# Filter spectrum first, kv spectrum second: swapping two transforms of an FFT-free long convolution and multiplying straight out of PSUM

## The chip, the cores and the metric

One core of one Trainium2 chip runs the whole program. The metric is the device time of one execution in microseconds (us); lower is better. Times are medians over several executions; the profile comes from one of them.

## The reference, cut to what matters

```python
def _A_ref(q, k, v, shift_k, ssm_k, ssm_D):           # S = 2048 rows, D = 576 columns
    k_shift = sum of 4 shifted copies of k, each times a row of shift_k
    kv = k_shift * v
    kv_f = rfft(pad(kv, 2*S), axis=rows)
    kf_f = rfft(pad(ssm_k, 2*S), axis=rows)            # the filter
    y = irfft(kv_f * kf_f)[:S].astype(bf16)
    return q * (y + kv * ssm_D)

h = layernorm(A_q) * (1 + ca) + sa                     # ca, sa, ... = silu(c) @ w_mod
x = A_q + ga * _A_ref(h, A_k, A_v, ...)
h = layernorm(x) * (1 + cb) + sb
x = x + gb * ((silu(h @ w1) * (h @ w3)) @ w2)          # F = 4608
```

The inputs are bf16. Both transforms need the same matrix of cosines and sines, 2048 x 2048 each.

## The kernel before, in words

The real FFTs are done as matrix products. Rows are cut into T = 16 blocks of 128 (index `a`, time) and 16 blocks of 128 frequencies (index `b`); a quad `bq` is four frequency blocks, 512 columns. The cosine and sine tiles `tq_c[a]`, `tq_s[a]` (128x512) are computed on the chip. One **generation**, for one `a` of one quad, is `gen1` and `gen2` (lines 124 to 141): ACT computes `g_y`; DVE computes `g_q`, `g_frs`, `g_m` and `g_frc`; ACT takes two sines into `tqx_s` and `tqx_c`. There are 4 x 16 = 64 generations. Each finished tile is also written to DRAM (`TC_dram`, `TS_dram`), from where the later stages load it again in halves of 128x256.

The stages follow one another on PE in this order.

1. Setup (lines 74 to 212): constants, the product `modps` of silu(c) with `w_mod`, its rows `B1row`, `A1row` and so on copied out of PSUM by DVE, then broadcast rows `skb`.
2. **X** (lines 282 to 348): the transform of `kv`. `x_gen(0)` makes the first quad's tiles. Then a loop over `a` makes `kv[:, a, :]` (lines 316 to 336): four loads `ktile`, four products and three additions on DVE, one load `vtile` from the POOL queue and a last product. `nyquist_pass(kv)` follows on PE, then `x_compute` for each quad: for each `b`, 64 matmuls of 288 columns accumulate into four PSUM tiles (`acc_c` and `acc_s`, two halves of D each, two buffers per tag, so all eight banks). DVE copies `acc_c` to `PX` and ACT copies `acc_s` to `SX` (lines 308 and 309). Generations of the next quad run under the matmuls, in a second buffer of tiles.
3. **LN1** (lines 354 to 363): the first layernorm, 16 rows of tiles, all on DVE with a square root on ACT, written to `H1_dram` from POOL.
4. **F** (lines 371 to 404): the transform of the filter. The filter is loaded transposed into `filtT` by 16 DMA transposes (lines 374 to 376), although an earlier `filtT` was loaded in the same way at lines 338 to 340; that first copy is read by nobody. `nyquist_pass(filtT)` follows, then for each pair of frequency blocks 32 loads of `tqf_c`, `tqf_s` from DRAM and 64 matmuls for each `b`. `pointwise` (lines 249 to 266) multiplies the two spectra: ACT scales the four PSUM tiles into bf16 `cfw`, `sfw`, and DVE makes six operations on 128x576 bf16 to give `YR` and `YI`.
5. The inverse transform (lines 408 to 452), with the gates, the second layernorm and writes to `H2_dram`.
6. The feed-forward part (lines 458 to 525).

A tile framework puts each engine's instructions into one fixed order, by priorities and a model of its own, and adds semaphore waits for data and for reused buffers. Each engine runs its list in order. DMAs are issued from the lists of SP, ACT or POOL; a DMA whose wait isn't met holds up all that stands behind it on that engine. Hardware-queue DMAs share eight completion semaphores in rotation, and software-queue DMAs (from POOL) another eight, so a DMA also waits for the one that used its semaphore before. PSUM and SBUF of a closed pool are reused by the next one, whose first writer waits for the old readers.

Of the kernel before, what the change touches and what calls it, by code (L numbers as in the profile page):

```python
# [20 lines left out]
def kernel(  # L21
# [26 lines left out]
    T = S // P  # L48
# [182 lines left out]
    filtT = fltp.tile([P, T, D], BF16, name="filtT")  # L231

# [16 lines left out]
    def pointwise(b, acc_c, acc_s, pw):  # L249
        wc = w_col0 if b == 0 else w_col  # L250
        cfw = pw.tile([P, D], BF16, name="cfw")
        sfw = pw.tile([P, D], BF16, name="sfw")
        for h in range(2):
            hs = slice(HOFF[h], HOFF[h] + HSZ[h])
            nc.scalar.activation(out=cfw[:, hs], in_=acc_c[h][:], func=ACT.Copy, scale=wc[:, 0:1])
            nc.scalar.activation(out=sfw[:, hs], in_=acc_s[h][:], func=ACT.Copy, scale=wc[:, 0:1])  # L256
        t1 = pw.tile([P, D], BF16, name="t1p")
        nc.vector.tensor_tensor(out=t1[:], in0=PX[:, b, :], in1=cfw[:], op=ALU.mult)
        t2 = pw.tile([P, D], BF16, name="t2p")
        nc.vector.tensor_tensor(out=t2[:], in0=SX[:, b, :], in1=sfw[:], op=ALU.mult)  # L260
        nc.vector.tensor_tensor(out=YR[:, b, :], in0=t1[:], in1=t2[:], op=ALU.subtract)
        t3 = pw.tile([P, D], BF16, name="t3p")
        nc.vector.tensor_tensor(out=t3[:], in0=PX[:, b, :], in1=sfw[:], op=ALU.mult)
        t4 = pw.tile([P, D], BF16, name="t4p")
        nc.vector.tensor_tensor(out=t4[:], in0=SX[:, b, :], in1=cfw[:], op=ALU.mult)
        nc.vector.tensor_tensor(out=YI[:, b, :], in0=t3[:], in1=t4[:], op=ALU.add)

# [14 lines left out]
    def x_gen(bq, tq_c, tq_s):  # L282
        frs_next = gen1(0, GWX * bq, GWX)
        for a in range(T):
            frs_cur = frs_next
            if a + 1 < T:
                frs_next = gen1(a + 1, GWX * bq, GWX)
            gen2(frs_cur, GWX, tq_c[a][:, :], tq_s[a][:, :])
            nc.scalar.dma_start(out=TC_dram[a, bq], in_=tq_c[a][:, :])
            nc.sync.dma_start(out=TS_dram[a, bq], in_=tq_s[a][:, :])  # L290

    def x_compute(bq, tq_c, tq_s, pp):
        for lb in range(QB):
            b = bq * QB + lb
            acc_c = [pp.tile([P, HSZ[h]], FP32, name="acc_c", tag=f"acc_c{h}") for h in range(2)]
            acc_s = [pp.tile([P, HSZ[h]], FP32, name="acc_s", tag=f"acc_s{h}") for h in range(2)]
            for a in range(T):
                lhs_c = tq_c[a][:, P * lb:P * lb + P]
                lhs_s = tq_s[a][:, P * lb:P * lb + P]
                for h in range(2):  # L300
                    nc.tensor.matmul(acc_c[h][:], lhs_c, kv[:, a, HOFF[h]:HOFF[h] + HSZ[h]],  # L301
                                     start=(a == 0), stop=(a == T - 1))
                    nc.tensor.matmul(acc_s[h][:], lhs_s, kv[:, a, HOFF[h]:HOFF[h] + HSZ[h]],  # L303
                                     start=(a == 0), stop=(a == T - 1))
            with tc.high_priority():
                for h in range(2):
                    hs = slice(HOFF[h], HOFF[h] + HSZ[h])
                    nc.vector.tensor_copy(out=PX[:, b, hs], in_=acc_c[h][:])
                    nc.scalar.copy(out=SX[:, b, hs], in_=acc_s[h][:])

    with tc.tile_pool(name="tqx", bufs=2) as tqx:
        tq_c0 = [tqx.tile([P, GWX], BF16, name=f"tqx_c{a}") for a in range(T)]
        tq_s0 = [tqx.tile([P, GWX], BF16, name=f"tqx_s{a}") for a in range(T)]
        x_gen(0, tq_c0, tq_s0)
        with tc.tile_pool(name="kvp", bufs=3) as kvp:
            for a in range(T):
# [17 lines left out]
                eng = nc.gpsimd  # L334
                eng.dma_start(out=vt[:], in_=v2[P * a:P * a + P, :])
                nc.vector.tensor_tensor(out=kv[:, a, :], in0=acc[:], in1=vt[:], op=ALU.mult)  # L336

        for a in range(T):
            eng = nc.sync if a % 2 == 0 else nc.scalar
            eng.dma_start_transpose(out=filtT[:, a, :], in_=A_ssm_k[:, P * a:P * a + P])  # L340
        nyquist_pass(kv, "kv", xnyq)
        with tc.tile_pool(name="ps_x", bufs=2, space=bass.MemoryType.PSUM) as pp:
            x_compute(0, tq_c0, tq_s0, pp)
            for bq in range(1, NBQ):
                tq_c = [tqx.tile([P, GWX], BF16, name=f"tqx_c{a}") for a in range(T)]
                tq_s = [tqx.tile([P, GWX], BF16, name=f"tqx_s{a}") for a in range(T)]
                x_gen(bq, tq_c, tq_s)
                x_compute(bq, tq_c, tq_s, pp)

    yr_pool = conv.enter_context(tc.tile_pool(name="yrp", bufs=1))  # L350
    YR = yr_pool.tile([P, T, D], BF16, name="YR")
    YI = yr_pool.tile([P, T, D], BF16, name="YI")

    with tc.tile_pool(name="ln1", bufs=3) as ln1p:
# [16 lines left out]
    with tc.tile_pool(name="fltp", bufs=1) as fltp, \  # L371
            tc.tile_pool(name="pw", bufs=2) as pw:
# [5 lines left out]
        with tc.tile_pool(name="tqf", bufs=1) as tqf, \  # L378
                tc.tile_pool(name="ps_f", bufs=2, space=bass.MemoryType.PSUM) as pp:
            for bbp in range(T // 2):  # L380
                tq_c = [tqf.tile([P, 2 * P], BF16, name=f"tqf_c{a}") for a in range(T)]
                tq_s = [tqf.tile([P, 2 * P], BF16, name=f"tqf_s{a}") for a in range(T)]
                bq, off = divmod(bbp, QB // 2)
                for a in range(T):
                    eng = nc.sync if a % 2 == 0 else nc.scalar
                    eng2 = nc.scalar if a % 2 == 0 else nc.sync
                    eng.dma_start(out=tq_c[a][:, :], in_=TC_dram[a, bq][:, 2 * P * off:2 * P * off + 2 * P])
                    eng2.dma_start(out=tq_s[a][:, :], in_=TS_dram[a, bq][:, 2 * P * off:2 * P * off + 2 * P])
                for e in range(2):
                    b = 2 * bbp + e  # L390
                    acc_c = [pp.tile([P, HSZ[h]], FP32, name="acc_c", tag=f"acc_c{h}") for h in range(2)]
                    acc_s = [pp.tile([P, HSZ[h]], FP32, name="acc_s", tag=f"acc_s{h}") for h in range(2)]
                    for a in range(T):
                        lhs_c = tq_c[a][:, P * e:P * e + P]
                        lhs_s = tq_s[a][:, P * e:P * e + P]
                        for h in range(2):
                            nc.tensor.matmul(acc_c[h][:], lhs_c, filtT[:, a, HOFF[h]:HOFF[h] + HSZ[h]],  # L397
                                             start=(a == 0), stop=(a == T - 1))
# [7 lines left out]
    px_pool_keep = None  # L406
# [149 lines left out]
```

## Time and profile before

| what | value |
|---|---|
| median of 6 runs | 1204.23 us (1203.07 to 1207.19) |
| the profiled execution, time | 1203.07 us |
| its span in the trace | 1201.3 us |
| PE busy | 951.3 us, 79% of the span |
| DVE busy | 551.4 us, 46% |
| ACT busy | 343.4 us, 29% |
| POOL busy | 37.4 us, 3% |
| first matmul of X, of F, of the inverse | at 131.30, 351.02, 479.56 us |

How to read the views: the timeline gives start, duration, engine, line and what an instruction waited for in brackets; "ACTq" and "SPq" are DMA issues on those queues. The windows view gives, for a stretch of the span, its length, the busy time of PE, weight loads, DVE, ACT and POOL with instruction counts, then the granted TensorE clock (1.00 is full), the share of the DMA engines that was busy and GB/s. The groups view gives busy time in total and the mean of one in ns, then the idle time before it and who ended it. The chain of waits is followed back from the last instruction. Instructions of one engine overlap a little, so a mean duration is longer than the distance from one start to the next.

### The profile page before, as it was taken

To read this page: it belongs to the slowest core of one execution; us is meant where nothing else is said; L and a number is where in the kernel's file an instruction comes from. 1 tells how busy PE (TensorE), PEld (TensorE's weight loads), DVE (VectorE), ACT (ScalarE), POOL (GpSimd) and SP (SyncE) were. 2 spreads that over 40 slices of the span, in tenths; PEclk is the share of its full clock that TensorE was granted. 3 is DMA by queue.
4 is the path that set the end of the run, shared out by engine and by line. 5 is a ranking of instruction groups with operands and counts; after the bars stand their busy time and mean duration, and the time that the engine had idled before them with its cause. 6 is when DMAs were issued, how large, how long until landed. Compare 5 with 4: busy or idle time off the path is not lost.

```text
span 1201.3 us, 15655 instructions
## 1 busy us (share of the span) xinstructions
PE 951.3 (79%) x5483; PEld 523.0 (44%) x5483; DVE 551.4 (46%) x1356; ACT 343.4 (29%) x613; POOL 37.4 (3%) x73
## 2 busy tenths in 40 slices
PE   5111699880149999999951899979999899999997
PEld 1000577660037777677740344433443344434442
DVE  3899999819003323456541233343333333353334
ACT  1641588711001222000000333323332233333331
POOL 1001000002000000000000000000000000000000
PEclk9555799985569999999985899989999899999998
DMA  9367533314215553676659111122111311121111
GB/s 216 113 184 214 159 115 102 118 34 128 59 35 141 141 141 87 191 209 194 189 175 350 47 41 44 45 67 65 40 45 48 86 41 45 43 76 45 45 40 50
DMA packets 169188, 126.43 MB, mean 105 GB/s; under 512 B 46423, under 2 KB 165203, under 8 KB 167828
## 3 DMA queue, kind: packets, MB, share of 16 engines
q1 hardware_dynamic: 84160, 58.48, 17.3%
q10 hardware_dynamic: 81876, 57.50, 16.6%
q0 software_dynamic: 3072, 9.44, 2.3%
q8 instruction: 43, 0.70, 0.2%
q14 instruction: 37, 0.30, 0.1%
HBM read 91.80 MB, written 26.21 MB: 98 GB/s over the span
## 4 chain that ended last, share of the span: by engine, by line
PE 56%; DMA 16%; DVE 13%; issue 12%; SPq 1%; ACT 1%; ACTq 1%; POOL 0%; DVEq 0%; POOLq 0%
PE gt L493 10%; PE outp L484 10%; PE ut L497 10%; PE acc_s L399 5%; PE acc_c L397 5%; PE iacc L431 5%; PE iacc L433 5%; DMA filtT<-in_A_ssm_k_dram 4%; DMA h2T<-H_dram 3%; DVE g_frs L132 3%; DMA ktile<-in_A_k_dram 2%; DVE g_frc L139 2%; PE acc_c L301 2%; PE acc_s L303 2%; DMA w1r<-in_B_w_dram 2%
## 5 line engine op out<-in xcount | busy, mean ns | idle before, releaser
L506 DVE TENSOR_TENSOR t_g<-gt,sig 128x512 bf16<-128x512 f32 x144 | 99.5, 691 | 271.2 <-ACT sig L502 270.8
L493 PE MATMUL gt<-h2T,w1r 128*128 128x512 bf16 x720 | 186.9, 387 | 41.7 <-DMA w1r<-in_B_w_dram 24.0
L497 PE MATMUL ut<-h2T,w3r 128*128 128x512 bf16 x720 | 186.7, 386 | 13.7 <-ACT upc L504 13.7
L484 PE MATMUL outp<-hh,w2t 128*128 128x512 bf16 (+1 forms) x720 | 195.2, 384 | 0.0
L502 ACT ACTIVATE sig<-gt 128x512 bf16<-128x512 f32 x144 | 86.0, 598 | 260.9 <-PE gt L493 238.2
L301 PE MATMUL acc_c<-kv,tqx_c 128*128 128x288 bf16 x512 | 129.2, 292 | 4.1 <-ACT tqx_c L141 3.3
L431 PE MATMUL iacc<-YR,tqi_c 128*128 128x288 bf16 x512 | 127.2, 287 | 3.8 <-ACT sfw L256 2.1
L303 PE MATMUL acc_s<-kv,tqx_s 128*128 128x288 bf16 x512 | 129.0, 291 | 0.0
L484 PEld LDWEIGHTS <-w2t 128*128 128x128 bf16 (+1 forms) x720 | 70.9, 100 | 129.1 <-issue 63.8
L433 PE MATMUL iacc<-YI,tqi_s 128*128 128x288 bf16 x512 | 126.8, 286 | 0.0
L397 PE MATMUL acc_c<-filtT,tqf_c 128*128 128x288 bf16 x512 | 126.2, 287 | 0.7 <-DVE fnyq L280 0.7
L399 PE MATMUL acc_s<-filtT,tqf_s 128*128 128x288 bf16 x512 | 126.1, 287 | 0.0
L493 PEld LDWEIGHTS <-w1r 128*128 128x128 bf16 x720 | 60.0, 99 | 124.8 <-issue 70.2
L497 PEld LDWEIGHTS <-w3r 128*128 128x128 bf16 x720 | 70.2, 99 | 99.5 <-issue 20.1
L504 ACT CAST upc<-ut 128x512 bf16<-128x512 f32 x144 | 84.5, 586 | 90.3 <-PE ut L497 88.2
L508 DVE TENSOR_TENSOR hh<-t_g,upc 128x512 bf16<-128x512 bf16 x144 | 61.2, 425 | 64.3 <-ACT upc L504 59.4
L276 PEld LDWEIGHTS <-nyq_col 128*1 128x1 bf16 x64 | 6.8, 108 | 166.2 <-issue 161.9
L276 PE MATMUL pnyq<-kv,nyq_col 128*1 128x288 bf16 x32 | 10.2, 422 | 77.3 <-DVE kv L336 77.3
L276 PE MATMUL pnyq<-filtT,nyq_col 128*1 128x288 bf16 x32 | 8.9, 434 | 76.7 <-DMA filtT<-in_A_ssm_k_dram 76.7
L128 ACT ACTIVATE g_y<-fiota,magic_col,tsc 128x512 f32<-128x512 f32 x64 | 51.1, 804 | 33.4 <-DMA filtT<-in_A_ssm_k_dram 19.0
L431 PEld LDWEIGHTS <-tqi_c 128*128 128x128 bf16 x512 | 49.9, 98 | 22.0 <-DMA tqi_c<-TC_dram 4.0
L301 PEld LDWEIGHTS <-tqx_c 128*128 128x128 bf16 x512 | 51.1, 100 | 18.4 <-ACT tqx_c L141 4.0
(111 smaller groups left out, 880.5 us busy)
## 6 DMA issues: line engine op xcount, KB each, us to landing
w2t<-in_B_w_dram SPq DMA_DIRECT2D x72, 144.0 KB, 2.1
w2t<-in_B_w_dram ACTq DMA_DIRECT2D x72, 144.0 KB, 2.1
TC_dram<-tqx_c ACTq DMA_DIRECT2D x64, 128.0 KB, 1.7
TS_dram<-tqx_s SPq DMA_DIRECT2D x64, 128.0 KB, 1.7
w3r<-in_B_w_dram ACTq DMA_DIRECT2D x5, 1152.0 KB, 9.9
w1r<-in_B_w_dram SPq DMA_DIRECT2D x5, 1152.0 KB, 19.3
ktile<-in_A_k_dram SPq DMA_DIRECT2D x31, 144.0 KB, 2.9
ktile<-in_A_k_dram ACTq DMA_DIRECT2D x30, 144.0 KB, 2.6
```

Source lines behind the costliest of these rows:

```text
L301: nc.tensor.matmul(acc_c[h][:], lhs_c, kv[:, a, HOFF[h]:HOFF[h] + HSZ[h]], start=(a == 0), stop=(a == T - 1))
L303: nc.tensor.matmul(acc_s[h][:], lhs_s, kv[:, a, HOFF[h]:HOFF[h] + HSZ[h]], start=(a == 0), stop=(a == T - 1))
L397: nc.tensor.matmul(acc_c[h][:], lhs_c, filtT[:, a, HOFF[h]:HOFF[h] + HSZ[h]], start=(a == 0), stop=(a == T - 1))
L399: nc.tensor.matmul(acc_s[h][:], lhs_s, filtT[:, a, HOFF[h]:HOFF[h] + HSZ[h]], start=(a == 0), stop=(a == T - 1))
L431: nc.tensor.matmul(acc[h][:], lhs_c, YR[:, b, HOFF[h]:HOFF[h] + HSZ[h]], start=(b == 0), stop=False)
L433: nc.tensor.matmul(acc[h][:], lhs_s, YI[:, b, HOFF[h]:HOFF[h] + HSZ[h]], start=False, stop=False)
L484: nc.tensor.matmul(outp[ci][:csz, :], w2t[:, c0:c0 + csz], hh[:, :], start=(fi == 0), stop=(fi == FC - 1))
L493: nc.tensor.matmul(gt[:, :], w1r[:, ci, P * ff:P * ff + P], h2T[:, ci, :], start=(ci == 0), stop=(ci == CCKn - 1))
L497: nc.tensor.matmul(ut[:, :], w3r[:, ci, P * ff:P * ff + P], h2T[:, ci, :], start=(ci == 0), stop=(ci == CCKn - 1))
L502: nc.scalar.activation(out=sig[:], in_=gt[:, :], func=ACT.Sigmoid)
L504: nc.scalar.copy(out=upc[:], in_=ut[:, :])
L506: nc.vector.tensor_tensor(out=t_g[:], in0=gt[:, :], in1=sig[:], op=ALU.mult)
```

## The change

F now comes first and X second, and what each stage does at its end is swapped.

- The 16 transposes of the filter are issued once, at the start of the convolution part, all from SP. The second `filtT` and its 16 transposes are gone.
- The generations now feed F (`f_gen`, `f_compute`). The writes of the tiles to `TC_dram`, `TS_dram` move from ACT and SP to POOL, 128 in all.
- F's PSUM tiles are scaled on the way out into `PFc`, `PFs`: one half of `acc_c` by DVE, the other three tiles by ACT.
- `kv` is made under F. X then runs with tiles loaded from DRAM, and its PSUM tiles are multiplied directly with `PFc`, `PFs` by DVE: 12 operations on 128x288, eight of which read PSUM, in place of 4 scalings on ACT and 6 operations of 128x576 on DVE.
- LN1's pool stays open, so that its instructions can stand among X's.
- The inverse and the feed-forward part keep their text.

The diff, cut to its core:

```diff
     fltp = conv.enter_context(tc.tile_pool(name="fltp", bufs=1))
     filtT = fltp.tile([P, T, D], BF16, name="filtT")
+    for a in range(T):
+        nc.sync.dma_start_transpose(out=filtT[:, a, :], in_=A_ssm_k[:, P * a:P * a + P])
...
-    def x_gen(bq, tq_c, tq_s):
+    def f_gen(bq, tq_c, tq_s):
...
-            nc.scalar.dma_start(out=TC_dram[a, bq], in_=tq_c[a][:, :])
-            nc.sync.dma_start(out=TS_dram[a, bq], in_=tq_s[a][:, :])
+            nc.gpsimd.dma_start(out=TC_dram[a, bq], in_=tq_c[a][:, :])
+            nc.gpsimd.dma_start(out=TS_dram[a, bq], in_=tq_s[a][:, :])
...
+                fwd_chunk_mm(filtT, tq_c[a][:, P * lb:P * lb + P], tq_s[a][:, P * lb:P * lb + P], acc_c, acc_s, a)
...
-                    nc.vector.tensor_copy(out=PX[:, b, hs], in_=acc_c[h][:])
-                    nc.scalar.copy(out=SX[:, b, hs], in_=acc_s[h][:])
+                    if h == 0:
+                        nc.vector.tensor_scalar(out=PFc[:, b, hs], in0=acc_c[h][:], scalar1=wc[:, 0:1], scalar2=None, op0=ALU.mult)
+                    else:
+                        nc.scalar.activation(out=PFc[:, b, hs], in_=acc_c[h][:], func=ACT.Copy, scale=wc[:, 0:1])
+                    nc.scalar.activation(out=PFs[:, b, hs], in_=acc_s[h][:], func=ACT.Copy, scale=wc[:, 0:1])
...
-        for a in range(T):
-            eng = nc.sync if a % 2 == 0 else nc.scalar
-            eng.dma_start_transpose(out=filtT[:, a, :], in_=A_ssm_k[:, P * a:P * a + P])
-        nyquist_pass(kv, "kv", xnyq)
+        nyquist_pass(filtT, "flt", fnyq)
...
-    with tc.tile_pool(name="ln1", bufs=3) as ln1p:
+    ln1p = conv.enter_context(tc.tile_pool(name="ln1", bufs=3))
...
-        filtT = fltp.tile([P, T, D], BF16, name="filtT")
-        for a in range(T):
-            eng = nc.sync if a % 2 == 0 else nc.scalar
-            eng.dma_start_transpose(out=filtT[:, a, :], in_=A_ssm_k[:, P * a:P * a + P])
-        nyquist_pass(filtT, "flt", fnyq)
...
+    nyquist_pass(kv, "kv", xnyq)
...
+                    fwd_chunk_mm(kv, tq_c[a][:, P * e:P * e + P], tq_s[a][:, P * e:P * e + P], acc_c, acc_s, a)
...
-                        pointwise(b, acc_c, acc_s, pw)
+                        t1 = pw.tile([P, HSZ[h]], BF16, name="t1p", tag=f"t1p{h}")
+                        nc.vector.tensor_tensor(out=t1[:], in0=acc_c[h][:], in1=PFc[:, b, hs], op=ALU.mult)
+                        t2 = pw.tile([P, HSZ[h]], BF16, name="t2p", tag=f"t2p{h}")
+                        nc.vector.tensor_tensor(out=t2[:], in0=acc_s[h][:], in1=PFs[:, b, hs], op=ALU.mult)
+                        nc.vector.tensor_tensor(out=YR[:, b, hs], in0=t1[:], in1=t2[:], op=ALU.subtract)
```

**ACT at the head of the program.** Before, in ACT's list from its sixth row on:

```order
L340 DMA_TRANSPOSE filtT<-in_A_ssm_k_dram 128x576 x5
L326 DMA ktile<-in_A_k_dram 127x576
L128 ACTIVATE g_y<-fiota,magic_col,tsc 128x512 x2
L326 DMA ktile<-in_A_k_dram 125x576
L128 ACTIVATE g_y<-fiota,magic_col,tsc 128x512
L340 DMA_TRANSPOSE filtT<-in_A_ssm_k_dram 128x576
L140 ACT_TABLE_LOAD
L140 ACTIVATE tqx_s_341<-g_frs 128x512
L141 ACTIVATE tqx_c_325<-g_frc 128x512
```

The same place now, again from the sixth row:

```order
L128 ACTIVATE g_y<-fiota,magic_col,tsc 128x512 x3
L140 ACT_TABLE_LOAD
L140 ACTIVATE tqf_s_354<-g_frs 128x512
L141 ACTIVATE tqf_c_338<-g_frc 128x512
L140 ACTIVATE tqf_s_355<-g_frs 128x512
L128 ACTIVATE g_y<-fiota,magic_col,tsc 128x512
L140 ACTIVATE tqf_s_356<-g_frs 128x512
L141 ACTIVATE tqf_c_339<-g_frc 128x512
```

The transposes, which stood ahead of the first table computations on ACT, are all on SP now, as 16 rows in a run ahead of SP's loads of `ktile`.

**DVE while kv is made.** Before, in the kv loop, DVE's list holds kv's products (L328 to L336) with generations between them, here behind the first finished row of kv:

```order
L336 TENSOR_TENSOR kv<-kacc,vtile 128x576
L137 TENSOR_SCALAR g_m<-g_frs 128x512
L130 TENSOR_SCALAR g_q<-g_y 128x512
L139 SCALAR_TENSOR_TENSOR g_frc<-g_frs,g_m 128x512
L132 SCALAR_TENSOR_TENSOR g_frs<-fiota,tsc,g_q 128x512
```

Now, in the loop (L315 to L322 are the same kv operations; L293 is the scaling of F's first block out of PSUM):

```order
L318 TENSOR_TENSOR ktmp<-ktile,skb_291 128x576
L319 TENSOR_TENSOR kacc<-kacc,ktmp 128x576
L130 TENSOR_SCALAR g_q<-g_y 128x512
L293 TENSOR_SCALAR PFc<-acc_c,w_col_312 128x288
L319 TENSOR_TENSOR kacc<-kacc,ktmp 128x576
L315 TENSOR_TENSOR kacc<-ktile,skb_270 128x576
L322 TENSOR_TENSOR kv<-kacc,vtile 128x576
```

The scalings of F's first four blocks now stand inside the kv loop, and DVE waits there for PE.

**DVE between the two transforms.** Before, after X's last copies, LN1 stands alone, and F's copy `fnyq` of the Nyquist row comes behind all of it:

```order
L308 CAST PX<-acc_c 128x288 x8
L241 BN_STATS stats_ln_2932<-xa 128x6 x2
L241 BN_STATS stats_ln_2947<-xa 128x6
L243 BN_AGGR mv_ln_2935<-stats_ln_2932 128x2
L241 BN_STATS stats_ln_2947<-xa 128x6
```

Now, after F's last four scalings; `xnyq` is the copy out of PSUM that X's first matmul waits for:

```order
L293 TENSOR_SCALAR PFc<-acc_c,w_col 128x288 x4
L242 BN_STATS stats_ln_2924<-xa 128x6 x2
L244 BN_AGGR mv_ln_2927<-stats_ln_2924 128x2
L242 BN_STATS stats_ln_2939<-xa 128x6 x2
L242 BN_STATS stats_ln_2954<-xa 128x6
L244 BN_AGGR mv_ln_2942<-stats_ln_2939 128x2
L242 BN_STATS stats_ln_2954<-xa 128x6
L247 RECIPROCAL rstd_ln_2929<-rstd_ln_2929 128x1
L262 COPY xnyq<-pnyq 1x288
```

And further on, where the first block of X is multiplied:

```order
L242 BN_STATS stats_ln_3014<-xa 128x6
L340 TENSOR_TENSOR h1t<-h1t,A1row 128x576
L377 TENSOR_TENSOR t1p<-acc_c,PFc 128x288
L379 TENSOR_TENSOR t2p<-acc_s,PFs 128x288
L382 TENSOR_TENSOR t3p<-acc_c,PFs 128x288
L380 TENSOR_TENSOR YR<-t1p,t2p 128x288
```

Five of LN1's 16 rows now stand ahead of the first product, and the other eleven between the products of the first six blocks; LN1 no longer ends before the second transform begins.

More of the change, by code (lines that the diff above doesn't have):

```diff
@@ L280, in nyquist_pass, with fwd_chunk_mm @@
                 nc.vector.tensor_copy(out=nyq_dst_row[0:1, HOFF[h]:HOFF[h] + HSZ[h]], in_=pn[h][0:1, :])
-    def x_gen(bq, tq_c, tq_s):
+    def fwd_chunk_mm(sig, lhs_c, lhs_s, acc_c, acc_s, a):
+        for h in range(2):
+            nc.tensor.matmul(acc_c[h][:], lhs_c, sig[:, a, HOFF[h]:HOFF[h] + HSZ[h]],
+                             start=(a == 0), stop=(a == T - 1))
+            nc.tensor.matmul(acc_s[h][:], lhs_s, sig[:, a, HOFF[h]:HOFF[h] + HSZ[h]],
+                             start=(a == 0), stop=(a == T - 1))
+    def f_gen(bq, tq_c, tq_s):
         frs_next = gen1(0, GWX * bq, GWX)
@@ L297, in x_compute @@
             for a in range(T):
[L298 to L304, printed above, removed]
+                fwd_chunk_mm(filtT, tq_c[a][:, P * lb:P * lb + P], tq_s[a][:, P * lb:P * lb + P], acc_c, acc_s, a)
+            wc = w_col0 if b == 0 else w_col
             with tc.high_priority():
```

115 lines of the change are left out of this document (47 added, 68 removed).

## The prediction

> **What bounds the kernel now.** I read the windows view first, with the span cut where PE's work changes. After start and length, the columns are busy us of PE, weight loads, DVE, ACT and POOL, then the granted clock, the DMA share and GB/s.
>
> ```profile
> span 1201.3 us, 15655 instructions
> 43.90:130.00 86.10, 9.67 (x31) 3.24 (x32) 81.94 (x201) 33.90 (x52) 6.99 (x13) 0.50 0.59 177
> 130.00:238.00 108.00, 103.90 (x831) 81.67 (x830) 101.78 (x202) 87.44 (x154) 0.00 (x0) 0.97 0.37 120
> 238.00:264.80 26.80, 26.75 (x196) 20.23 (x194) 2.94 (x8) 2.36 (x7) 0.00 (x0) 0.90 0.13 36
> 264.80:304.00 39.20, 0.00 (x0) 0.00 (x0) 33.35 (x114) 6.45 (x19) 8.30 (x16) 0.53 0.38 117
> 304.00:351.00 47.00, 8.95 (x32) 3.70 (x33) 0.81 (x2) 0.00 (x0) 0.37 (x1) 0.50 0.24 53
> 351.00:477.40 126.40, 126.38 (x1024) 100.45 (x1023) 35.73 (x92) 25.41 (x61) 0.00 (x0) 0.99 0.42 118
> ```
>
> From 43.9 to 130 DVE is the limit (generations and kv). From 130 to 238 PE and DVE both are nearly full (X). From 238 to 264.8 PE finishes X alone. Then PE stands still: 39.2 us for LN1 on DVE, and 47 us in which neither DVE nor ACT works. F, from 351.0 to 477.4, is PE at full rate: 1024 matmuls in 126.4 us, 7.9 us for each of 16 blocks. The chain of waits says what the 47 us are (start, length, what):
>
> ```profile
> 306.24 2.72 DMA filtT<-in_A_ssm_k_dram
> ...
> 346.58 2.61 DMA filtT<-in_A_ssm_k_dram
> ...
> 350.16 0.82 DVE fnyq L280 x2
> 351.02 0.40 PE acc_c L397
> ```
>
> Sixteen transposes, one after another, 2.65 us apart. The head has a second delay of this kind, seen in the timeline:
>
> ```profile
> 16.11 11.89 PE L179 MATMUL modps<-wmodt,silubc 64*128 64x512 bf16 x31 [0.47 <-DMA wmodt<-in_w_mod_dram]
> 30.22 1.15 ACTq L340 DMA_TRANSPOSE filtT<-in_A_ssm_k_dram  x1
> 32.69 0.63 ACT L140 ACTIVATE tqx_s<-g_frs 128x512 bf16<-128x512 f32 x1
> 34.62 0.75 DVE L181 CAST B1row<-modps 128x576 bf16<-128x576 f32 x1
> ```
>
> ACT's first sine waits behind a transpose on its own queue, DVE waits for that sine, and so takes `B1row` out of PSUM at 34.62, though `modps` was done at 16.11 + 11.89 = 28.0.
>
> **The change, part by part.** I go by time and count what each checkpoint moves.
>
> *Head.* Without transposes on ACT, DVE can take `B1row` when `modps` ends, about 28.1: 6.5 us earlier. All setup copies follow it as before, so the stretch that starts at 43.9 starts at 37.4. One thing can eat this: ACT's load of `ktile`, now just ahead of its fourth sine, shares a semaphore with the tenth transpose on SP. If SP's transposes run at 2.65 us each from 16.1 (when the last weights land), the tenth is down at 16.1 + 10 x 2.65 = 42.6 and most of the 6.5 us is gone. In the first pass the queue was quicker:
>
> ```profile
> 19.86 16.75 SPq L340 DMA_TRANSPOSE filtT<-in_A_ssm_k_dram  x8
> ```
>
> Eight issues in 16.75 us, 2.1 each, with ACT's between them; at that rate the tenth is down near 37, when DVE needs it. I take 6.5; the bounds are 1 and 6.5.
>
> *Generations, kv, F on PE.* The work on DVE is all still there, in another order: kv loop, then generations with F following. From 43.9 to the last sine DVE's list took 237.8 - 43.9 = 193.9 us:
>
> ```profile
> L132 DVE SCALAR_TENSOR_TENSOR g_frs<-fiota,tsc,g_q 128x512 f32<-128x512 f32 x43 | 32.1, 747 | 0.8
> L139 DVE SCALAR_TENSOR_TENSOR g_frc<-g_frs,g_m 128x512 f32<-128x512 f32 x45 | 30.9, 687 | 1.1
> L308 DVE CAST PX<-acc_c 128x288 bf16<-128x288 f32 x24 | 9.8, 450 | 0.8 <-PE acc_c L301 0.8
> 237.14 0.63 ACT L141 ACTIVATE tqx_c<-g_frc 128x512 bf16<-128x512 f32 x1 [0.56 <-DVE g_frc L139]
> 237.80 0.33 ACTq L289 DMA_DIRECT2D TC_dram<-tqx_c  x1
> ```
>
> (These rows are for 130 to 238.) DVE has 24 casts there; now it has one scaling for each of the 12 blocks that end before the last sine, so 12 go: 12 x 0.41 = 4.9 us. In order, DVE is one `g_frs` and one `g_frc` further when the setup copies end: 1.3 us at their distance of 0.66 and 0.60. DVE was idle for 108 - 101.78 = 6.2 us, partly behind PE, partly behind ACT, which spent 0.33 us per generation issuing `TC_dram` writes; those are now on POOL. I take 4.5 of the 6.2. Against that: kv's first row waits for a `ktile` load that stands behind the first quad's last sine on ACT (2.5, about one load's landing), and at a quad's end the last sine stands behind ACT's copies of two blocks (2.0 in all). Net 6.2 us shorter; bounds -4 (DVE waits in the kv loop for PE to end blocks 0 to 3, which start cold) and 12 (all the idle time back, no new wait). What is issued on POOL is hidden as long as POOL keeps up (a rival, below).
>
> *F's tail.* Before, 264.8 - 237.8 = 27.0 us of PE followed the last sine: three blocks and the throttled clock of 0.90. PE's list now takes blocks 12 and 13 along with the generations, so two blocks and a fourth of one are left: 2.25 x 7.9 = 17.8 us. 9.2 us shorter, if PE is still at full clock; at half clock for one block 7.9 us of it are lost.
>
> *Between the transforms.* Gone are LN1's 39.2 us and the 47.0 us: from X's end to F's first matmul were 351.0 - 264.8 = 86.2 us. What replaces it: the input load for LN1 shares memory with F's tiles and so waits for F's end; DVE's list puts LN1's first statistics and a square root from ACT ahead of the copy `xnyq`, for which X's first matmul waits. The nearest rows are the same steps before:
>
> ```profile
> 264.83 27.54 SPq L358 DMA_DIRECT2D xa<-in_A_q_dram  x8
> 267.91 1.18 DVE L241 BATCH_NORM_STATS2 stats_ln<-xa 128x6 f32<-128x288 bf16 x3 [2.67 <-DMA xa<-in_A_q_dram]
> 270.23 0.15 DVE L246 RECIPROCAL rstd_ln<-rstd_ln 128x1 f32<-128x1 f32 x1
> ```
>
> 5.4 us from load to reciprocal, then two copies, 0.82 (the `fnyq` row), with a second normalized row between them, about 1: some 7.2. X's 32 tile loads start only now too, and behind waits of LN1 in both queues; I add 1.3 for PE catching up with them. 8.5 us in place of 86.2: 77.7 us saved. Bounds of the new gap 5.4 and 13.
>
> *X itself.* PE's work is F's 126.4 us. DVE's is new. The products with a PSUM operand have a twin in the inverse stage, all-SBUF ones too, and LN1's rows are known:
>
> ```profile
> L443 DVE TENSOR_TENSOR u_upd<-u_upd,iacc 128x288 bf16<-128x288 bf16 x32 | 14.6, 455 | 38.9 <-PE iacc L438 37.0
> L445 DVE TENSOR_TENSOR u_upd<-u_upd,G1row 128x288 bf16<-128x288 bf16 x32 | 8.3, 302 | 0.0
> L241 DVE BATCH_NORM_STATS2 stats_ln<-xa 128x6 f32<-128x288 bf16 x32 | 13.4, 437 | 4.8 <-DMA xa<-in_A_q_dram 4.7
> L247 DVE TENSOR_SCALAR h1t<-xa,mv_ln,rstd_ln 128x576 bf16<-128x576 bf16 x16 | 6.8, 424 | 0.2
> L361 DVE TENSOR_TENSOR h1t<-h1t,A1row 128x576 bf16<-128x576 bf16 x16 | 7.2, 451 | 0.0
> ```
>
> A block costs DVE 8 x 0.455 + 4 x 0.302 = 4.85 us against PE's 7.9. LN1's 33.35 us of busy time, 2.1 a row, lie among them: five rows ahead, eleven between the first six blocks. Those blocks then need 4.85 + 2.2 x 2.1 = 9.5 us of DVE for 7.9 of PE, 1.6 too much over five gaps: 8 us, which the second PSUM buffer (one block, 7.9 us) takes up. The ten later blocks have 3 us to spare each. I take 3 us for X's stalls, bounds 0 and 18.
>
> *Into the inverse.* Its first matmul waited 2.14 us for ACT's scalings; now it waits for DVE's whole last block:
>
> ```profile
> 479.56 0.65 PE L431 MATMUL iacc<-YR,tqi_c 128*128 128x288 bf16 x4 [2.14 <-ACT sfw L256]
> ```
>
> At 4.85 instead of 2.14 that is 2.7 later, but the tile loads, which bind just after, gain that time; I take 1. The rest keeps its text and its order.
>
> **Sum**: 6.5 + 6.2 + 9.2 + 77.7 - 3 - 1 = 95.6 us. The profiled execution took 1203.07 us (span 1201.3 and 1.8 around it), so 1107.5; the median of the runs lies 1.2 above it: **1108.7 us**.
>
> **POOL, where a rule of the skill speaks against the change.** 128 writes go to POOL's queue, and DVE is nearly always busy while they are issued. Before, POOL wrote LN1's rows from SBUF to DRAM in the stretch where DVE was busy 33.35 of 39.2 us; group row, and the landing from the page's DMA issues:
>
> ```profile
> L363 POOL DMA_DIRECT2D H_dram<-h1t x16 | 8.7, 542 | 175.7 <-DMA xa<-in_A_q_dram 152.7 <-DVE h1t L362 17.8 <-DVE mv_ln L243 4.6
> H_dram<-h1t POOLq DMA_DIRECT2D x16, 144.0 KB, 2.1
> ```
>
> 0.54 us an issue, 2.1 us to landing. A generation of about 2.08 us asks for two writes, so POOL may take 1.04 each, twice what it took. The Trainium skill (SBUF — State Buffer, section "SBUF: two separate sides") says that DMAs from the POOL queue have their descriptors written by GpSimd, which is locked out while DVE runs in a mode with both ports, and gives about 3.1 us instead of 0.62 for such a transfer (section "A bandwidth-pool intuition that's wrong"). By that rule the sum would be estimated as 96 x (3.1 - 1.04) = 198 us worse, 1307 us. The rows above don't show it, and they have a DVE operation with one tensor in them (L247); `g_q` and `g_m` on fp32, which will stand beside the new writes, they don't have.
>
> **The rivals.**
>
> *POOL falls behind* (5%, the slower side). Each write is done alone, to landing, before the next is served: 2.1 us. For the 96 writes of quads 1 to 3, whose generations run without kv's work between them, that is 96 x (2.1 - 1.04) = 102 us late; LN1's first load and X's first tiles wait for the last of them: 1108.7 + 102 = 1210.5 us, slower than before. It decides from 1.04 + 95.6 / 96 = 2.04 us a write. For it: a tile is never reused before its write has landed. Against it: eight semaphores let eight writes be under way, and 0.54 us above.
>
> *DVE binds the first half of X* (11%). DVE's rows of LN1 wait for ACT's square root, which stands in ACT's list behind tile loads that wait for PE to read the old tile; DVE then waits half a block with full PSUM buffers. At up to 4 us for each of the five gaps, less 3 counted already: 18 us to 1127 us.
>
> *LN1 is not hidden*, so the change does only half of what it says (5%). If X's matmuls wait until LN1 is through, 39.2 us less the 3 come back: 1145 us. Against it: X's first matmul waits for `xnyq`, which stands ahead of most of LN1.
>
> **How the numbers follow.** The forecast has 79%. Its slow end: 5.5 at the head, 5 in F, 5 at the tail or the gap, 7 in X make 22: 1131, which takes in the second rival. Its fast end: 6 from DVE's idle time, 3 from the gap, 3 from X, 6 from a quicker kv loop make 18: 1091. Outside 1091 to 1131 lie the other two rivals and a tenth of the forecast. What a measurement can tell from no change is about 0.2%, 2.4 us. Faster: 0.94; the first rival and mishaps of its size make 0.05 slower; 0.01 for the same.
>
> **What would show it.** Right: `B1row` near 28; the last sine near 225, F's last matmul near 243, X's first near 251, the inverse's first near 385; no idle time above 10 us on PE between F and the inverse; POOL's writes at 0.54 us. Wrong: POOL busy above 1 us a write with ACT waiting for it; DVE idle behind ACT's square root in X with PE waiting for DVE; or DVE waiting long for PE in the kv loop.

## The result, and the profile after

The changed kernel takes **1098.8 us** (median of 8 runs, 1098.2 to 1102.0) against 1204.4 for the kernel before (16 runs): a ratio of 0.9127, with a 95% interval of 0.9115 to 0.9139. That is 105.6 us less; the forecast was 95.5 less, 1108.7. The profiled execution took 1099.3, with a span of 1097.2 us.

The windows view of the changed kernel, cut at the checkpoints that the prediction named; columns as there:

```profile
span 1097.2 us, 15698 instructions
25.40:60.00 34.60, 11.55 (x68) 6.22 (x68) 33.42 (x78) 24.60 (x38) 13.55 (x25) 0.62 0.74 129
60.00:116.00 56.00, 36.34 (x272) 27.41 (x271) 51.10 (x133) 10.00 (x19) 9.71 (x18) 0.80 0.72 205
116.00:212.50 96.50, 81.87 (x600) 55.14 (x601) 95.98 (x201) 91.22 (x160) 53.09 (x91) 0.95 0.36 125
212.50:231.40 18.90, 18.87 (x154) 14.69 (x151) 1.92 (x4) 3.94 (x10) 0.71 (x2) 1.00 0.07 23
231.40:237.90 6.50, 4.12 (x33) 2.81 (x34) 4.02 (x15) 2.92 (x6) 0.00 (x0) 1.00 0.63 182
237.90:373.10 135.20, 127.35 (x1024) 99.07 (x1024) 92.87 (x294) 4.14 (x14) 8.72 (x16) 1.00 0.54 156
```

Up to 212.5 DVE is the limit, and from 116 on it has no gap to speak of (95.98 of 96.50). Then PE ends F alone, 6.5 us separate the transforms, and X takes 135.3 us up to the inverse, 6.7 more than the 128.5 that F took to the same point before. Of the 86.2 us between the transforms 6.5 are left. The timeline rows at the checkpoints:

```profile
5.48 28.28 SPq L232 DMA_TRANSPOSE filtT<-in_A_ssm_k_dram  x16
15.77 9.64 PE L179 MATMUL modps<-wmodt,silubc 64*128 64x512 bf16 x31 [0.77 <-DMA wmodt<-in_w_mod_dram]
25.45 0.76 DVE L181 CAST B1row<-modps 128x576 bf16<-128x576 f32 x1 [9.42 <-PE modps L179]
...
212.50 0.62 ACT L141 ACTIVATE tqf_c<-g_frc 128x512 bf16<-128x512 f32 x1
...
231.08 0.29 PE L268 MATMUL acc_s<-filtT,tqf_s 128*128 128x288 bf16 x1
232.49 4.08 PE L258 MATMUL pnyq<-kv,nyq_col 128*1 128x288 bf16 x32 [1.13 <-ACT PFs L296]
237.86 0.28 PE L266 MATMUL acc_c<-kv,tqx_c 128*128 128x288 bf16 x1 [1.28 <-DVE xnyq L262]
...
373.13 0.28 PE L412 MATMUL iacc<-YR,tqi_c 128*128 128x288 bf16 x1 [3.39 <-DVE t4p L384]
```

Each stretch is taken from one checkpoint to the next, in both profiles:

| stretch (ends with) | before, us | after, us | saved | forecast |
|---|---|---|---|---|
| head (`B1row` starts) | 34.62 | 25.45 | 9.2 | 6.5 |
| generations and kv (last sine starts) | 202.5 | 187.1 | **15.5** | **6.2** |
| tail of the first transform (its last matmul ends) | 27.7 | 18.9 | 8.8 | 9.2 |
| between the transforms (first matmul) | 86.2 | 6.5 | 79.7 | 77.7 |
| second transform (first matmul of the inverse) | 128.5 | 135.3 | -6.7 | -4 |
| all the rest | 721.7 | 724.0 | -2.3 | 0 |

But for rounding these add to the 104.1 us by which the spans differ. The rest has the same instructions in both kernels, in the same order but for a dozen matmuls and a few DMAs at its start; over the 14 profiles of this study it lies between 718.8 and 724.2, so its 2.3 us lie within that scatter. The largest miss is the generations. The theory to test is what saved the other 9 us there.

**The theory of neighbours.** DVE's list in the kernel before has two orders of a generation. Its timeline, first under X near 152, then near 163:

```profile
151.52 0.42 DVE L130 TENSOR_SCALAR g_q<-g_y 128x512 f32<-128x512 f32 x1
151.98 0.75 DVE L132 SCALAR_TENSOR_TENSOR g_frs<-fiota,tsc,g_q 128x512 f32<-128x512 f32 x1
152.76 0.43 DVE L137 TENSOR_SCALAR g_m<-g_frs 128x512 f32<-128x512 f32 x1
153.22 0.69 DVE L139 SCALAR_TENSOR_TENSOR g_frc<-g_frs,g_m 128x512 f32<-128x512 f32 x1
153.83 0.42 DVE L130 TENSOR_SCALAR g_q<-g_y 128x512 f32<-128x512 f32 x1
...
162.54 0.42 DVE L130 TENSOR_SCALAR g_q<-g_y 128x512 f32<-128x512 f32 x1
162.88 0.42 DVE L137 TENSOR_SCALAR g_m<-g_frs 128x512 f32<-128x512 f32 x1
163.21 0.74 DVE L132 SCALAR_TENSOR_TENSOR g_frs<-fiota,tsc,g_q 128x512 f32<-128x512 f32 x1
163.87 0.68 DVE L139 SCALAR_TENSOR_TENSOR g_frc<-g_frs,g_m 128x512 f32<-128x512 f32 x1
164.47 0.42 DVE L137 TENSOR_SCALAR g_m<-g_frs 128x512 f32<-128x512 f32 x1
```

In the first piece each operation reads what the one ahead of it wrote, and the generation takes 2.31 us from `g_q` to `g_q`. In the second the neighbours belong to different generations, and the same four operations take 1.93. An instruction that doesn't need its neighbour starts about 0.08 us before that one ends (0.34 and 0.66 us apart at lengths of 0.42 and 0.74); one that does starts 0.03 us after its end (0.46 and 0.78). So a dependent neighbour costs 0.12 us; over all pairs of neighbours from the generations before, the medians are 0.035 us after the end for 79 dependent ones and 0.083 before it for 133 others. The changed kernel's list holds 2 dependent ones: 77 x 0.12 = **9.2 us**. Between the same two points DVE also has fewer rows (12 scalings in place of 24 casts, one `g_q` and one `g_m` less, three small ones more), about 4.5 us by their start-to-start distances, and its other idle time is some 2 us shorter. Together that is about the 15.5 measured. The rival: DVE was held by PE and ACT under X, and its own order cost nothing.

### The profile page after: what moved, and what is told of

It is laid out like the page before. It is cut to its first block, busy times and chain, and to the rows that moved or that the text cites. A ratio compares the mean times of both kernels' runs of the same rounds, so it can differ in the third digit from the quotient of the medians.

```text
span 1097.2 us, 15698 instructions
## 1 busy us (share of the span) xinstructions
PE 950.0 (87%) x5483; PEld 516.8 (47%) x5483; DVE 564.8 (51%) x1436; ACT 323.5 (29%) x565; POOL 110.7 (10%) x201
## 4 chain that ended last, share of the span: by engine, by line
PE 57%; issue 14%; DMA 14%; DVE 10%; POOL 2%; ACT 1%; ACTq 1%; SPq 1%; POOLq 0%; DVEq 0%
PE gt L474 12%; PE outp L465 11%; PE ut L478 11%; PE iacc L412 5%; PE acc_s L268 5%; PE acc_c L266 5%; PE iacc L414 5%; DMA h2T<-H_dram 3%; DMA ktile<-in_A_k_dram 3%; DMA w1r<-in_B_w_dram 2%; DVE g_frc L139 2%; DMA tqi_c<-TC_dram 2%; DVE g_frs L132 1%; DMA tqx_s<-TS_dram 1%; DMA wmodt<-in_w_mod_dram 1%
## 5 line engine op out<-in xcount | busy, mean ns | idle before, releaser
L483 ACT ACTIVATE sig<-gt 128x512 bf16<-128x512 f32 x144 | 86.0, 598 | 262.5 <-PE gt L474 239.6
L266 PE MATMUL acc_c<-filtT,tqf_c 128*128 128x288 bf16 x512 | 119.8, 292 | 43.9 <-DVE fnyq L262 26.2
L266 PE MATMUL acc_c<-kv,tqx_c 128*128 128x288 bf16 x512 | 126.0, 286 | 3.3 <-DMA tqx_c<-TC_dram 1.9
L268 PE MATMUL acc_s<-filtT,tqf_s 128*128 128x288 bf16 x512 | 120.7, 293 | 8.9 <-ACT tqf_s L140 8.7
L268 PE MATMUL acc_s<-kv,tqx_s 128*128 128x288 bf16 x512 | 126.0, 286 | 2.5 <-DMA tqx_s<-TS_dram 2.4
L246 ACT ACTIVATE rstd_ln<-mv_ln,eps_col 128x1 f32<-128x1 f32 x32 | 9.5, 296 | 268.8 <-DMA h1a<-H_dram 135.7
L268 PEld LDWEIGHTS <-tqf_s 128*128 128x128 bf16 x512 | 48.9, 99 | 59.5 <-issue 31.1
L500 POOL DMA_DIRECT2D x1f<-out_dram x16 | 8.6, 539 | 574.1 <-DVE ostage L505 561.4
L266 PEld LDWEIGHTS <-tqf_c 128*128 128x128 bf16 x512 | 48.7, 99 | 33.1 <-ACT tqf_c L141 20.4
L128 ACT ACTIVATE g_y<-fiota,magic_col,tsc 128x512 f32<-128x512 f32 x64 | 51.2, 806 | 25.4 <-DVE g_q L130 19.7
## 6 DMA issues: line engine op xcount, KB each, us to landing
w3r<-in_B_w_dram ACTq DMA_DIRECT2D x5, 1152.0 KB, 10.4
```

The lines of the kernel that those rows point to most:

```text
L128: nc.scalar.activation(out=y[:], in_=fj, func=ACT.Identity, bias=magic_col[:], scale=tcol)
L266: nc.tensor.matmul(acc_c[h][:], lhs_c, sig[:, a, HOFF[h]:HOFF[h] + HSZ[h]], start=(a == 0), stop=(a == T - 1))
L268: nc.tensor.matmul(acc_s[h][:], lhs_s, sig[:, a, HOFF[h]:HOFF[h] + HSZ[h]], start=(a == 0), stop=(a == T - 1))
L483: nc.scalar.activation(out=sig[:], in_=gt[:, :], func=ACT.Sigmoid)
```

## The experiments

Every number of time is the median of 4 or 5 runs; ratios are to the kernel before, on the same chip.

**1. Dependent order forced** (x_chain). `g_q` and `g_m` share one buffer:

```diff
-        q = genp.tile([P, width], FP32, name="g_q")
+        q = genp.tile([P, width], FP32, name="g_q", tag="g_qm", bufs=1)
...
-        m = genp.tile([P, width], FP32, name="g_m")
+        m = genp.tile([P, width], FP32, name="g_m", tag="g_qm", bufs=1)
```

> The changed kernel, with g_q and g_m in one shared buffer, so that DVE's list must go q, frs, m, frc in 48 of the 64 generations. All work stays. The theory of neighbours: an operation on DVE that stands right behind the one whose result it reads starts 0.12 us later than otherwise (0.78 and 0.46 from start to start, against 0.66 and 0.34, in the two orders that the trace of before holds). 96 such neighbours in place of 2 give 11 us more, 1110; if waiting for the shared buffer to be read counts in the same way, there are twice as many and it is 22 more, 1121. The rival, that DVE's slower stretch under X came from waiting for PE and ACT and not from its own order: 1099, no change.

Measured: 1127.7 us, ratio 0.9361 (0.9343 to 0.9379), 28.9 more than the changed kernel. Its timeline:

```profile
131.93 0.43 DVE L130 TENSOR_SCALAR g_q<-g_y 128x512 f32<-128x512 f32 x1
132.46 0.75 DVE L132 SCALAR_TENSOR_TENSOR g_frs<-fiota,tsc,g_q 128x512 f32<-128x512 f32 x1
133.25 0.43 DVE L137 TENSOR_SCALAR g_m<-g_frs 128x512 f32<-128x512 f32 x1
133.79 0.69 DVE L139 SCALAR_TENSOR_TENSOR g_frc<-g_frs,g_m 128x512 f32<-128x512 f32 x1
134.59 0.43 DVE L130 TENSOR_SCALAR g_q<-g_y 128x512 f32<-128x512 f32 x1
```

No row waits for another engine, the durations are the same, and the generation takes 2.66 us in place of 1.93. The rival falls: order, with the waits that come with it and all work unchanged, is worth this much. The forecast of 1110 or 1121 was too low. Waiting for a buffer to be read counts like waiting for data, and where every instruction waits, three of the four steps cost 0.19 to 0.20 more and one 0.13. 48 x 0.73 = 35 us is just how much later the last sine starts (247.6 against 212.5); F's tail is 3.4 shorter in return.

**2. Tile writes back on ACT and SP** (x_hwq).

```diff
-            nc.gpsimd.dma_start(out=TC_dram[a, bq], in_=tq_c[a][:, :])
-            nc.gpsimd.dma_start(out=TS_dram[a, bq], in_=tq_s[a][:, :])
+            nc.scalar.dma_start(out=TC_dram[a, bq], in_=tq_c[a][:, :])
+            nc.sync.dma_start(out=TS_dram[a, bq], in_=tq_s[a][:, :])
```

> The changed kernel with the writes of the tiles back on ACT and SP. With ACT's issues in its model the scheduler puts 89 dependent neighbours into DVE's list (2 in the changed kernel, 79 before). The theory of neighbours: 87 x 0.12 = 10.4 us more, 1109, and up to 8 more if ACT with its 64 issues of 0.33 us becomes the one that DVE waits for. The rival, that the queue of the writes alone matters (POOL's writes cost DVE something): the time falls below 1099. If neither matters, 1099.

Measured: 1109.2 us, ratio 0.9209 (0.9196 to 0.9223), 10.3 more. DVE's waits in it from 116 to 235 (total, times, longest):

```profile
DVE PFc L293 <- PE acc_c L266: 7.3, 3, 2.4
DVE g_q L130 <- ACT g_y L128: 0.5, 2, 0.3
```

The last `g_frc` starts 16.6 us later than in the changed kernel (228.3 against 211.6). 87 pairs x 0.12 make 10.4 of it, and 4.9 are the first two of the waits for PE (the third comes after that row): the scheduler, with ACT's DMA issues in its list, also places the scalings where PE is not done. The last sine stands behind ACT's scalings and is 17.9 later. F's tail is 3.4 shorter in return, since PE has caught up by then, and the rest of the program 4.4, within its scatter. The end agrees with the 10.4 foretold, but partly because these cancel.

**3. All tile writes on SP** (x_spq): as in 2, with both writes from `nc.sync`.

> The changed kernel with all 128 writes of the tiles on SP, so neither on ACT nor on POOL. DVE's list keeps 2 dependent neighbours. The theory of neighbours: 1099 within 3 us, since the order on DVE is that of the changed kernel. The rival, that it is the hardware queue that costs what the other run with ACT and SP will show: the same time as that run, about 1109. If POOL's writes hurt DVE: below 1097.

Measured: 1098.6 us, ratio 0.9125 (0.9103 to 0.9146): the changed kernel's time. So no cost of POOL's writes or of the hardware queues shows; what costs is the order that comes of having the issues in ACT's list.

**4. The kernel before with its tile writes on POOL** (x_before_pool): the edit of 2 in the other direction.

> The kernel before with its 128 writes of tiles moved to POOL and nothing else. DVE's dependent neighbours fall from 79 to 1. The theory of neighbours: DVE saves 9.4 us under X, but PE, which starts X at 131 and needs 126.4 us for it, allows 264.8 - 131.3 - 126.4 = 7 us at most; 6 us faster, 1198. The rival, that DVE was held by PE and ACT there: 1204, no change, X's end at 264 to 265.

Measured: 1199.1 us, ratio 0.9953 (0.9934 to 0.9973), 5.4 less. The last sine comes 13.4 us earlier (223.7), X's end only 6.9 (257.9). The window under X shows why:

```profile
130.50:237.00 106.50, 106.50 (x856) 84.39 (x856) 94.10 (x200) 90.09 (x155) 48.80 (x88) 0.98 0.39 130
```

PE is busy for the whole window. From `B1row` to the last sine it is 14.6 us shorter: 78 pairs fewer at 0.12 make 9.4, DVE's waits for `g_y` and `ktile`, 5.4 before, are 1.5 here, and four casts come after the last `g_frc`. The head is 1.2 later, and of the 13.4 left PE allowed half. In the changed kernel F starts under kv's loop (at 67.7) and PE has room, so that the order counts.

**5. As 2, without the look-ahead of one row in each generation** (x_hwq_25_fewer).

```diff
-        frs_next = gen1(0, GWX * bq, GWX)
         for a in range(T):
-            frs_cur = frs_next
-            if a + 1 < T:
-                frs_next = gen1(a + 1, GWX * bq, GWX)
+            frs_cur = gen1(a, GWX * bq, GWX)
             gen2(frs_cur, GWX, tq_c[a][:, :], tq_s[a][:, :])
```

> The changed kernel with the tile writes on ACT and SP, as in the run with 89 dependent neighbours (1109.2), but with each generation written without the look-ahead by one row, which leaves the same operations and gives 64 such neighbours. The theory of neighbours: 25 x 0.12 = 3 us faster than that run, 1106. The rival, that the 10 us of that run are ACT's 64 issues and not the order on DVE: 1109, no change.

Measured: 1115.8 us, ratio 0.9263 (0.9248 to 0.9277): 6.6 slower than run 2 where 3 faster was expected. A miss of both sides. DVE's waits from 116 to 235:

```profile
DVE g_q L130 <- ACT g_y L128: 8.7, 7, 1.4
DVE PFc L290 <- PE acc_c L266: 5.0, 4, 2.5
```

With fewer pairs the list has a new wait: DVE for ACT's `g_y`. 62 pairs more than in the changed kernel make 7.4, and the waits ahead of the last `g_frc` 8.7 and 3.7 (one of 1.3 for PE comes after it): 19.8 of the 21.3 us by which that row is later (232.9). So the price of a pair holds within 1.5 us here, and within 1.3 in run 2, but a count of pairs does not rank two orders by itself.

**6. The kernel before with one set of transposes** (x_before_onefilt): the second `filtT` and its 16 transposes are deleted.

> The kernel before without its second set of 16 transposes: F reads the first filtT. The theory that the 47 us from 304 to 351 were these transposes and nothing else: F's first matmul follows the end of LN1, 42 to 47 us earlier, 1157 to 1162. If F then also starts under LN1, as it reads nothing of it, up to 16 us more (two blocks into the two PSUM buffers): 1141. The rival, that tile loads and the Nyquist pass would have taken most of these 47 us anyway: 1185 or above.

Measured: 1156.0 us, ratio 0.9588 (0.9567 to 0.961), 49.3 less. F starts under LN1 at 272.4, but PE's waits hold one long one:

```profile
PE acc_c L392 <- ACT cfw L255: 23.6, 1, 23.6
```

After two blocks PE waits for ACT's scalings, which stand behind LN1's square roots in ACT's list, and these follow DVE. So the 47 us were the transposes, and of the 16 us that F could have gained under LN1 it kept about 2. A second transform hides LN1 only if what empties PSUM isn't queued behind LN1.

**7. Transposes on SP and ACT in turn** (x_split).

```diff
-        nc.sync.dma_start_transpose(out=filtT[:, a, :], in_=A_ssm_k[:, P * a:P * a + P])
+        eng = nc.sync if a % 2 == 0 else nc.scalar
+        eng.dma_start_transpose(out=filtT[:, a, :], in_=A_ssm_k[:, P * a:P * a + P])
```

> The changed kernel with the 16 transposes of the filter on SP and ACT in turn, eight of them in ACT's list ahead of its first table row. The theory that ACT's own queue made the late head before: B1row moves from 25.4 back to 34 or later and the time grows by 9 to 12 us, 1108 to 1111. The rival, that the head is covered by later work (kv's loads, PE): 1099 to 1101.

Measured: 1114.6 us, ratio 0.9248 (0.9234 to 0.9263), 15.8 more. ACT's timeline:

```profile
14.97 18.76 ACTq L233 DMA_TRANSPOSE filtT<-in_A_ssm_k_dram  x5
33.78 2.22 ACT L128 ACTIVATE g_y<-fiota,magic_col,tsc 128x512 f32<-128x512 f32 x3 [30.64 <-issue]
```

(The window begins at 15; all eight of ACT's issues, from 3.0 on, stand ahead of its first row, more than before.) `B1row` moves from 25.4 to 39.6, by 14.2; the last sine comes 18.4 later and the end 15.8. So nothing covers the head.

**8. LN1's pool closed before X** (x_ln_first): `YR`, `YI` and then LN1 in a `with` block of its own, as in the kernel before.

> The changed kernel with LN1's pool closed again before X, so that X's tiles take its memory. The theory that the open pool is what hides LN1: X's first matmul waits until LN1 is nearly through, 33 to 39 us later, less the 5 us of stalls that X has now; 1127 to 1133. The rival, that LN1 is hidden by its place in DVE's list alone, whatever its pool: 1099 to 1103.

Measured: 1132.4 us, ratio 0.9392 (0.9378 to 0.9406), 33.6 more. PE's waits:

```profile
PE acc_c L266 <- DMA tqx_s<-TS_dram: 37.9, 1, 37.9
```

X's tiles take the memory of LN1's pool, so their loads wait until LN1 is through. X itself, with no row of LN1 under it, then waits for no tile load, though its first one is issued only 2.9 us ahead. The one line that keeps the pool open is what hides LN1.

**9. X's products by way of ACT** (x_act_pw): ACT copies the four PSUM tiles of X to bf16, DVE multiplies in six operations of 128x576.

> The changed kernel with X's PSUM tiles copied to bf16 by ACT and multiplied by DVE in six operations of 128x576, as F's were before. DVE then needs 6 x 0.45 = 2.7 us a block in place of 4.9, ACT four copies. The theory that X's pace is set by PE and by the loads of its tiles: 1097 to 1101, since DVE had room; the last block's DVE time ahead of the inverse shrinks by about 1, and ACT's copies stand ahead of tile loads in its queue, which can cost 1 to 4. The rival, that DVE with LN1 and the products bound the first half of X: 1092 to 1095.

Measured: 1099.6 us, ratio 0.9123 (0.9106 to 0.9139): no difference. PE's waits in X are still for tile loads:

```profile
PE acc_s L268 <- DMA tqx_s<-TS_dram: 4.2, 3, 2.1
PE iacc L416 <- ACT sx L379: 1.9, 1, 1.9
```

The wait ahead of the inverse falls from 3.4 to 1.9, and those for tile loads grow from 4.3 to 4.9 in all. DVE doesn't bind X; no gain of multiplying straight out of PSUM shows here.

**10. LN1 written at the end of F** (x_ln_under), in memory that kv's loads have left.

```diff
                 f_compute(bq, tq_c, tq_s, pp)
+        with tc.tile_pool(name="ln1", bufs=3) as ln1p:
+            for a in range(T):
...
-    ln1p = conv.enter_context(tc.tile_pool(name="ln1", bufs=3))
```

> The changed kernel with LN1 written (and its pool placed) at the end of F, in memory that kv's loads have left, so that its rows can run in DVE's idle time under F's last blocks (DVE was busy 1.7 of the 18.2 us there) and its loads no longer wait for F's tiles. The theory that X's start waits for LN1's first rows and X's stalls come from LN1's loads among its tile loads: the gap between the transforms falls from 6.7 to about 5.5, the stalls in X from 4.3 to 1 or 2; 3 to 5 us faster, 1094 to 1096. The rival, that the stalls come from the tile loads by themselves: 1097 to 1099. If LN1's rows delay DVE's scalings of F, slower than 1099.

Measured: 1104.1 us, ratio 0.9164 (0.9148 to 0.9181), 5.2 slower. ACT and PE at the end of F:

```profile
235.60 0.29 ACT L246 ACTIVATE rstd_ln<-mv_ln,eps_col 128x1 f32<-128x1 f32 x1 [2.27 <-DVE mv_ln L244]
235.80 0.48 ACT L296 ACTIVATE PFs<-acc_s,w_col 128x288 bf16<-128x288 f32 x1
...
237.11 4.08 PE L258 MATMUL pnyq<-kv,nyq_col 128*1 128x288 bf16 x32 [3.70 <-DVE h1t L248]
246.85 0.40 PE L266 MATMUL acc_c<-kv,tqx_c 128*128 128x288 bf16 x1 [5.66 <-DVE xnyq L262]
```

Half of the theory holds: X has no stall for tile loads any more (128.3 us from its first matmul to the end of its last, 131.9 in the changed kernel). But F's last scalings and `xnyq` now stand behind LN1's rows, and the gap between the transforms is 13.4 us in place of 6.5. What was to make a better version made a worse one.

**11. Every tile written twice from POOL** (x_pool_twice), the second time to a buffer that nobody reads.

> The changed kernel with every tile written twice by POOL, the second time to a DRAM buffer that nobody reads: 256 writes. The theory that a write costs POOL its 0.58 us and no more: four take 2.3 us, 0.4 more than a generation's 1.93, so POOL falls behind by at most 48 x 0.4 = 19 us and the time is 1105 to 1118. The rival of the prediction, that a write is served only when the one before it has landed (2.1 us): it would have shown in the changed kernel, and here four writes take 8.4 us a generation, over 1300.

Measured: 1110.1 us, ratio 0.9212 (0.9199 to 0.9224), 11.3 more, inside the forecast range, but by another sum. POOL does fall behind: it issues its last write at 239.6, 19 us after the last sine starts. F's tail covers that but for a gap before X that is 3.0 longer. Of the rest, 2.3 are a later end of `modps` (`B1row` at 27.75), and 5.5 are DVE's longer waits for `ktile` loads (10.4 against 4.9). A write took POOL 0.60 us on average, so the rival of serial writes, at 2.1, falls.

**12. The kernel before with both repairs, 4 and 6** (x_before_both).

> The kernel before with the tile writes on POOL and without its second set of transposes, still with X first and F second. If the two gains measured alone (5.4 and 49.3 us) add up: 1150. What is left to the changed kernel's 1099 is then the swap itself: LN1 under X, 34 us by the run with LN1 ahead of X, and the head, 9 to 16 us, which add to 43 to 50.

Measured: 1151.7 us, ratio 0.9557 (0.9543 to 0.9571). The two gains add up: 53.3 of 54.7. The changed kernel is another 52.9 faster. By the checkpoints of the two profiles 11.3 of it lie in the head, 2.9 in the generations, 15.3 in the tail of the first transform (F's first matmul runs under kv's loop, at 67.7, X's here only after it, at 133.5) and 24.6 in the gap and the second transform, where LN1 is hidden. Runs 7 and 8, at 15.8 and 33.6, put more on the head and on LN1 than the step from this kernel gains there. So half of the change's gain needs no swap of the transforms.

## Why the prediction was right, and where it was off

*Between the transforms*, 77.7 of 95.6: right in mechanism and size (79.7). Runs 6 and 8 show its two parts, 49.3 and 33.6 us; the pool that stays open decides the second.

*Head*, 6.5 against 9.2: right in mechanism (run 7). The 2.7 missing are `modps`: its last 31 matmuls took 11.89 us in the one profile of before, 9.4 to 10.0 in eleven others of this study, and 10.5 and 11.8 in those of runs 8 and 11. The forecast took `B1row`'s new start from the first; the 2.7 are this scatter, and luck. `modps` was never waited for in the kernel before, so nothing showed the value as odd.

*Generations, kv, F on PE*, 6.2 against 15.5: **the step that failed**, with a result outside its own bounds of -4 and 12. "The work on DVE is all still there, in another order" put nothing on the order itself: the gain was 12 casts, the list's first instructions and 4.5 of 6.2 us of idle time "partly behind PE, partly behind ACT". The waits of DVE before, from 130 to 237, name only 2.4 us behind those two:

```profile
DVE g_q L130 <- ACT g_y L128: 1.6, 2, 1.4
DVE PX L308 <- PE acc_c L301: 0.8, 1, 0.8
```

Another 2.9 of the 6.2 are 78 gaps of 0.03 to 0.04 us behind dependent neighbours, and the larger part of their price, the lost overlap, is in the busy column. The two paces, 2.31 and 1.93, stood in the timeline of before, and the pairs could be counted in the order. The waits feared for PE in the kv loop and behind ACT's copies at a quad's end did not come in any size; the new sine is where the fewer rows, the fewer pairs and the shorter idle time put it.

*F's tail*, 9.2 against 8.8, and at full clock (1.00): right.

*X*, -3 and -1 against -6.7. The size was near, the reason was not. The stalls were put down to DVE with LN1 among its products, but PE's waits in X are these:

```profile
PE iacc L412 <- DVE t4p L384: 3.4, 1, 3.4
PE acc_s L268 <- DMA tqx_s<-TS_dram: 2.4, 4, 1.7
PE acc_c L266 <- DMA tqx_c<-TC_dram: 1.9, 3, 0.7
```

Until X's last matmul 4.3 us go to tile loads and none to DVE (run 9). In runs 8 and 10, where all of LN1's loads are issued before X's first matmul, these waits are gone. That points to LN1's rows in the lists that issue the tile loads; whether its own loads or its square roots on ACT hold them up stays open. DVE's cost for a block was right, as a row of its group in X shows, x32 with 455 ns forecast:

```profile
L377 DVE TENSOR_TENSOR t1p<-acc_c,PFc 128x288 bf16<-128x288 f32 x32 | 14.5, 452 | 36.0 <-PE acc_c L266 36.0
```

*POOL falls behind*: it did not. Groups and landing in the changed kernel:

```profile
L278 POOL DMA_DIRECT2D TC_dram<-tqf_c x64 | 38.1, 596 | 25.4 <-ACT tqf_c L141 23.6 <-issue 0.2
L279 POOL DMA_DIRECT2D TS_dram<-tqf_s x64 | 35.5, 555 | 69.1 <-ACT tqf_s L140 64.1 <-ACT tqf_c L141 4.8
```

```profile
TC_dram<-tqf_c POOLq DMA_DIRECT2D x64, 128.0 KB, 2.0
```

0.58 us each, far from the 2.04 at which this rival decides, while DVE was busy for 95.98 of 96.50 us. The rule of the Trainium skill (SBUF — State Buffer, "SBUF: two separate sides", with the figures of "A bandwidth-pool intuition that's wrong") would have given an estimated 1307; with the writes on SP the time is the same (run 3), so no price of it shows here.

The other two rivals: DVE did not bind the first half of X, and LN1 was hidden. In X DVE waited for LN1's square roots for 4.0 us in all and 1.1 at most, where the former rival had up to 4 for each of five gaps (less the 3 counted that is 17, not 18). Run 6 shows a mechanism of its kind in the kernel before, at 23.6 us: scalings on ACT queued behind LN1's square roots.

## What to carry to other kernels

Where an engine is the limit, count in its list the instructions that stand right behind what they wait for; their price shows only in part as idle time (about 2.9 of 9.2 us here), and a harmless edit elsewhere (which queue issues a DMA) can reorder the list by way of the scheduler. Price a stage by start-to-start distances rather than by busy and idle, and from more than one profile where a duration was never waited for. Whether a stage hides under the next is decided by memory and by what stands behind it in each list: a pool that stays open was worth 34 us, and moving LN1 into idle time one stage earlier cost 5.

## What the runs showed of the hardware

Among the fp32 operations of 128x512 here, DVE starts an instruction about 0.08 us before the one ahead ends if it doesn't wait for it, and 0.03 us after its end if it does; where all of them wait for one another (run 1), 0.10 to 0.11 after it at most steps. The Trainium skill (VectorE: DVE Perf Modes, "The DRAIN you can't avoid") reports that eight copies on DVE took the same time with a semaphore after each as with one after the last. No run here repeats that; here it was the dependent order that cost 0.38 us on a 1.93 us generation, and 0.73 in run 1. The 128 writes issued from POOL, most of them beside a DVE that was busy for 95.98 of 96.50 us, took 0.54 us at the median and 1.15 at most.
